# Attention and two expert layers on one core: four more score tiles turned by DMA, and a new written-out order of work

## The chip, the cores and the metric

One core of a Trainium2 chip runs one program. The metric is the device time of one execution in microseconds (us); it is compared as a median of several executions.

## What is computed

The reference first does clustered attention for 2 batches, 8 heads, 768 positions, head size 64, and then two dense layers on the 1,536 tokens.

```python
mask = q_assign[:, :, :, None] == k_assign[:, :, None, :]
scores = scale * np.matmul(q, k.transpose(0, 1, 3, 2))
scores = np.where(mask, scores, -1000000000.0)
scores = scores - np.max(scores, axis=-1, keepdims=True)
attn = np.exp(scores)
attn = attn / (np.sum(attn, axis=-1, keepdims=True) + 1e-09)
return np.matmul(attn, v).astype(np.float32)
...
h = x @ w_in
g = np.where(pos, h, np.where(neg, 0.0, (h + beta) ** 2 / (4.0 * beta)))
return (g @ w_out).astype(np.float32)
...
a = x @ w1
b = x @ w2
h = a * b @ w3
return (h @ w_out).astype(np.float32)
```

`q_assign` and `k_assign` are the nearest of 16 cluster centres; the mask lets a query see the keys of its own cluster alone.

## The kernel before, in words

**The score tiles.** The two batches of attention run one after the other. Each batch has 4 pairs of heads (units), each unit two groups of queries `g`, each group 2 heads `h` with 3 tiles `t` of 128 queries by 768 keys: 48 tiles a batch, numbered `s`, 0 to 47 and 48 to 95. One tile goes through these steps:

- `s` on TensorE (`s_mm`, L846 to L855): eight matmuls into a PSUM bank pair of the ring `sc`.
- `smax` on VectorE (`s_max`, L861), `sbias` on GpSimd (L866), `sexp` on ScalarE (`s_exp`, L874).
- The tile must then be turned, so that keys lie on partitions. `by_pe(s)` (L883) says how. If it is true, `spT` on TensorE (`s_pT`, L891) turns it as six blocks of 128 by 128 into the same bank, and then `shi` (ScalarE or VectorE, `copy`, L347 or L349) writes the upper half in f16 into `pt`, and `sT` on VectorE (`s_lo`, L352) the lower half. If it is false, `shi` and `slo` first write the two f16 halves into a buffer `phl`, and `sT` (`s_T`, L921) turns both by one DMA issued on SyncE's queue (SP) into `pt`.
- `pv` (L962 in the first batch, L970 in the second) multiplies the six turned tiles of a group with the values.

In batch 0 every tile is turned by TensorE, in f32. In batch 1 it is every sixth, that is `h = 0, t = 0` of each of the eight groups: tiles 48, 54, 60, 66, 72, 78, 84 and 90.

**Buffers.** In batch 1 the ring `sc` has two members (L175), so a tile's matmuls wait for the lower half (`slo`, or `sT` on VectorE) of the tile two before it. The ring `phl` has two buffers (L211 and L213); the values `v` of each unit use it too (`vh`, `vlo`, `vT` L772). A buffer of `phl` is free again when its DMA has landed.

**The rest.** While batch 1 of the attention runs, TensorE also does the dense layers of the first batch's tokens (steps `h`, `y`, `ab`, `o`: `mm4`, L1254, twelve matmuls each), and VectorE, ScalarE and GpSimd rebuild 64-bit weights into f32 (L1107 to L1140) and split values into two parts. SP carries the put-back of rebuilt weights (`wd<-wf`, L1143), loads of q, k and v, and all DMA turns. After the attention only dense layers are left (L1254, L1507).

**The order.** Every step is one `plan.add(...)`, 3,072 in all. `Plan.order` (L126) does not plan: it reads the string `ORDER`, two letters a step, which give the step's number and which of its allowed engines runs it. The steps are emitted in that order, and every engine and every DMA queue works strictly in order. So the string alone sets the order on each engine, and the costs and due times in the `add` calls are not used when the kernel is built.

```python
            i, alt = divmod(LETTERS.index(a) * len(LETTERS) + LETTERS.index(b), 2)
            name, engines, _, fn, needs, _, _, prev, _, _ = self.ops[i]
            out.append((fn, list(engines)[alt], name, 0.0))
...
    def by_pe(s):
        return s % PE_EVERY[s // NU] == 0
...
                if by_pe(s):
                    add(("spT", s), {"PE": 0.655}, p + 3.0, s_pT(s, b), [("sexp", s), "c_put"], frees=[(("P", b), s)], near=(("sc", b), s))
                    add(("shi", s), hi, p + 3.5, s_hi(s, u, g, h, t), [("spT", s)], first, behind=key)
                    add(("sT", s), lo, p + 4.2, s_lo(s, u, g, h, t), [("shi", s)], frees=[(("sc", b), s)])
                    continue
                add(("shi", s), hi, p + 3.3, s_hi(s, u, g, h, t), [("sexp", s)], [(("phl", b), s)])
                add(("slo", s), lo, p + 4.0, s_lo(s, u, g, h, t), [("shi", s)], frees=[(("sc", b), s)])
```

Of the kernel before, what the change touches and what calls it, by code (L numbers as in the profile page):

```python
# [35 lines left out]

LETTERS = "#$%&()*+,-./0123456789:;<=>?@ABCDEFGHIJKLMNOPQRSTUVWXYZ[]^_`abcdefghijklmnopqrstuvwxyz|~"
ORDER = (
    "##$V$.$0$4#%#*$X$2#,#0$]#.$Z%s%X%V%Z#(%e#2#4%h%k$6%c$_%y&,%r:m%_$H$8%m$::|$a;.$<%a;<$q%|$c$>%i#_$J&%#i#e$e%u"
# [4 lines left out]
    "+a&G+e+u*s+g&/+V+c,(<g&=,4<L+m,*&4<N<w+w%@<o,6+y,,+|<:,8<i,.<<,@,:<>,#<y<|,<,%<@,0<]<k,L,2<_<P=*,B=:,N,>,D,F"
    ",P=#=%,R&I=(,X<a,H<m<c,u,J<q+i=L,w-4+k&J,Z,y=,<s-6,]=],|+o-8=.=k,_=0=2&N=4,T,W&D-#=6,e=<&T,a-(&Q,g=N=8,c-*-%"
    "=>-,+r=_=|+s-.=a=@&@-:=P=B-@=D-<&B=R-0=F=V=c=T,m&_=H-B=X&Z-2-D>4->=e=g&L&S=i>D&W-L=J=m-F-X=p&c,i-N&k-u&X,l-H"
    "-Z&o=Z&j>R-]=u=q-P-_=s-R-K=w,o-a>#-w>6-T=y>%-V-y>(,q>*-|>,>.-c>8,s%>&e>F>T>H>:>>.(><&].#.*>]-m>V.%.,>X>c>u>Z"
    ">0>J..&b>L-e.0&g>N-g.4>P.@%B>@.6%(-i%%.L-k>_>2.2>B.N?%.B.P.8.:.<-o.D&u&n.F>e>w.H?,.X>z.R>a.Z.J>g?:?J.].>>i._"
    ">k>m.T>q>|.u>o.V.e%*?#.a?]>s?(/(.w?D/4&r.c.g?*/*&y?.($/,&w?0&~-q-s(,?<?m/@/..m/B(%/6?L.y%,((?2/8?4.|%D?N/:?P"
    "?6?_/#?R?8/</%?>/0?@&s?T%./2?B?V/>?a?F?g%F%0?|%2/D/F?H?c?o%H@2@D%4?e?i?q/H?X/L/J?Z%6%J.i.k/N/P/X@,?k.o(*%L/R"  # L50
    "/Z@#.q%N/]/_@%/T.s/e/a/V@(?s%P@T/c%8?u/u?w0(%:@*@.?y/m@4%R%</w%T@6/y@8/g/|0*@F0,04@V@H0#0@06@c@N@:08@00%@J0:"
    "@<@X@>0.@L(.@Z@P0B00@A@m0<@]@s@B/i02@_0LA,/l@a@e0X0N@R0Z0P0R@g0]0?A<0D@i0_@k0T/o@o0a0F0u/q@u0H0w@q0J@w@yAJ0V"
    "0e0d0gA./sA>@|0y0|A#A@1((0A%AB(41#(2A0(61LA6AL0mADAF1*1%1,A2A4A8A(1.10A*ANAH1NAZAP1PAR14120i16AT1@F40l1X180o"
    "AV1:A:1B(:1Z1D(8(=1]1F(A0q1H(>A]1<(DA_AX1?1_AaAm1RAc(BAe1e1JAg(M1g1TB2(HAj1a(N1W1c1iAo2*(G0s1uArBPF>1m2,(J1w"
    "2.20(PAk1y1|2#22B5Bo24BRAs1kBT2%261o1r1s(R28Au(ZB62((TB%(VAx2:(X2FB(AyB+B8A|2<B,C42>B/2HB0Bc2@2JB:2BB<2L2DB>"
    "BDBACR2NBCBrBe2P2TBgB$BV2RBiBFBtC62VBHCq2cBXBJ2XBlB[2ZC(2eBm2]D%2_2gBuFPC8FkB]2i2aCUB_3%2kBa(]CFC*3(CVC,2mBw"
    "By3*C.2o34CsB|3,BMC:BO36CHD4CKC#Cv3.38CX30CLC%C<32C>CNC@3B3:2qC1CwC3D(3<3D(_3FDBCe(gCz3>3H3@3J(a(c3PDP2y3RCZ"
    "3L3TC]CgD+3ND6C_3VD8CB3X3mC|Ci3ZD#D,(i(l3](nCk3_(e3oD03a3q3sD/3c(tDoD>3eDE(u3gDGDLCQFu3|E42sD23iCn3k3vCoD:DN"
    "DR3wD@Cb3yDUCc4>DqD=ER2u(o4@404BDc424D(qCE44(w4FDsDH464H4#De(yDg2xEq48E62|4L4:4JE9DV4NF%F6Di3#4PF8F:Dl4%DX4*"
    "F<DZDKETF@4<4R4)Dm4TD]D_EVE(4V(|4,4XFR)#DuE*FTG>4.FVDb)%FX4ZEsFZE,4iEu4]DwF]E:Gi)(DyE.4_D|4aE$4kEX4cE14mE<4e"  # L60
    "E2FmE>4gEFFoEZFqE&E]4oE@FBFsEe)*4qF)E_F*EH4sEJ5:FwEg4uEa4w5<EiFDEcE|ELFyG@4y5>5@EkFGEwEB4|5#EEGB5%GD5,5BGFF_"
    "F0F#5DFaEyH<Gk5F5.GsGH5VGmF,GJ5(Hg),Go5*).Gq5H5XF|GuENFL5J5LH>GwF2Em5ZF.H@FHG$G2EQ)1HqHiHBFNGL)2I*Hk5NEpHDFg"
    "G4HF5]FJ5PHmHoFc5_5RHsG6IDG85TFiGNG%Gy5a)5HHI,5cIa5eHJI.G~G:GPHLG(5gHuG*FeIF5iG,IN5sIH5kI0IJ50G]ILGRI2GTIP52"
    "5uG.5m54I45wHw5oI6Hy5yGVI|G1GXJN6(5q5|H#6*G_)6G=6,GaG[)@H0H%Gc56H(6#Ic58IeJ#)BH|IgIRH2H*J,IiI8GfIkH46DGg)8H6"
    "ImHN6F6.H-Jy6HI#606%66HZJ%HPH/6J62I;I%J(JP);HRITJR)<J*IV6RHTH]6L6TH_)>I<J.I(Ha)DHc6VJ06N68I@646X6ZHe6PHVJTKD"
    "JV6aIoJXIXH86]IqJ2KgI>J|6_6c)F6oIBIs6eIZJZ6gK#K%6iJ5I]K*K(KF6qK,6kJ6KiH;6mKkIuL2KqJ]KH6s6u7#J`K.6>7%J86wJ;I_"
    "6yHXKJJ<7(7*7N6|KLIwKm7,KNLTKoKP7PKsL4Ja7.7RK1707TK3JcL6L8Je)NIy)HKuJgL:LqJi)JJBJDJk7V72J>JFJm6:)LKRJH7XJAKT"
    "7Z)PK4Jo74JJJqL<6<76JsL>7]KVJMJu6@L_JwK6LVK8LX78LZK_K:KwL]7:KXLaM:7<LsK<KyKa7>7_KcKZMV7a7kK]L@7@7cK|LBK>KeK@"
    "7m7eKBM<7oLD7B7g7qM>)TLuM@)R7yLFLwLeL*6BLy7sLc7iL|MDMBM#7HL#MyMF7|L%7uLgN<L(MX7wLI8#LLMZL,M]MHL.LJM%M_8%8.M("
    "L0LN7D8(Li7G)VMJ8*LPM|LR8,8<MaLkMLN>Lm7J)_807L)XN@82NBM*84N#N%N_Mc)bMeN*86M2N(M,N,Lo8>)])[MN8@N.N|888BMh8:8g"  # L70
    "8DNDMRM.NFN0M0M48iODMPN2Na8FNJMU8k8HNcNMMqMiO#Ne)h)cNiO%M6N88X)eMs8mNgNkMkO(8Z)iM8NmNoNV8JNHN:8o8]O*MmONMoN4"
    "8qOF8_OHO,MuNr8uOaMwN6NX8a8wNZ8RO0OJOL8yP*8c8s8L8|)kO29#NN8eOc9%Oe9(9*N^P,NP8NNw8PP.P0OPPF9,9.ORO.8TOgOi90Ns"
    "9F)m)oOk92)qOmO48VOTNS)sPiNyNUP4O<OWP2P6Nu9H9496OXO69JPHPJPLP8PN98OZOoPPO]Q,9LO>O9Or9NP;P=O|OsQNPT9PPkPsPV9:"
    "O_Pm9<Po9>PqOu9@PXO@9BP#9DPuQkQ.OC9cPyQ1P>9eP%9RQPOwQR9g9qP@9TPROy9iPwPZPaO;QXP|Q2PBQ49s9k9uQ(9mQ6Q89VQ:9o9w"
    "Q=:%P]QTQm9]QV9yQoQZPD9|R4:#P_:4:(:*PcPeP(Q#:6Q]:,PgQq:8Q>Q%QsQ*Q_Qu:.QbQwQyQF:0::Q|Q@:2QB:<:BQHR>Qc:>R6:D:@"
    "R9:F:P9XQK:H9[Qg9_9aQeRPRZ:JQE:R:TR#R@:L:VRB:NQiQLR,R%:Y:ZR:RRR.:]R(RT:_RmRwR*R<R1R2RDR^:a:cRF:g:eRJSNRp:iSR"
    "SPRH:kRXRLR`SLRNSyRVSVS|T#S]S0S:SrRrT%RgSURyS`SXTLSaT)RsT4SfT6SjRaSgRjSnR~RuS2T0S5T8SpTNRcT+S#ReSdTDStT;S<T<"
    "U_S?UaS%T3T-T@S(T/RkTUS*TGTWTYTZT?S6S8TPT^SlTaTeTSTiTdS,VqTqTnUcS.TIUhUoTKSFTlUjVsT`TCUfTsSHUlU%UnThS@X*UsTp"
    "S[U(UuSuSCU6VvSDVzTyTuU8SJSxUxU:UyTwU*U<V|U,V2U|VwV%U.W(U0V*X/U@U>V.UBW#UDT|V$W%V9X,UFU#U2UqY<W,V<UJX0V(W<V>"
    "ULUHU4V0W1UTW+W2UNXNW4UVV@W6VBV,X2UXYJVRW.V4WDV:VTUQX4VHURUZX6VJU]W8V6VLX:X<X>VVWJW@VDVXXAXBVZV]WFVFY>V`WNX]"  # L80
    "WBVNVaWPVcY@XPVPVgVeViW>X9XDVkYXXFWVXRVmWRWoWTYBWrVoWeWLXIWZYMXJX_YFYNWgXaYgXmWsYuW;W^YZWiYPYHWuWwXpYwWkY]W_"
    "WmWaXVXqXLYjXsYTWcYkXuXcZ#XTYyZ&Z(Z,YDWHZ+Z0Z2YcWXXeY|WyZ5[.[0W|Y_Z9Z<Z6Z/YRXgZ;XwZDX#]@X%XyXX]NX|Ye[2XiY#X("
    "[4Y(Y%YVY*YqY,[7[9[?[BYbZ@YmYt]B[;[<Y/[R]]YoXZZN[@ZRZH[FY0XkZ?[D[VY2]EY4[IZFY6ZTY8ZB[aY:[K]F]Q[LZP[e]k]S]yZ_"
    "ZV[TZX[OZi[ZZaZlZc]JZmZo]_]|]X]nZf]oZg[c]b[q]T[Q]HZq^)[X^#]Z[s^+^,_2^0ZJ[u^%[wZL[y_4ZZ]c[gZsZ]Zu]V[#^5^9[&]L"
    "[]Zw^.[iZy]u[m^:[k_;[|],]#[(]q]._=^<]%`D^>]0]([*_>^2]*]g^@Z|^6]3_C[,]s^D_6]w_8`F[_]4_G_@^L]e[o^B^H]i]6^R_I]8"
    "`I_V`R_J`a_M`J]:]=_f]>^F_E^V`L^J`T`W_X_O_P^T`N_S^c^X_T`oa#a2^e^N`P_g^Z`X_u^]`c_x^g`f`q`]_y^m^jae^p^q`ga%^__|"
    "^ka(^s^w^u^y`t`k`_as`ZbL`i^|_Z`#_#a4_%___ia7_a`mbNbT_k_]_c_m_o^P_q_s`0`u`%`2`(`4bV`*`6^a`yb]`8_(bY`:_+`-`<b`"
    "a8b[bbbe_,bi`>bkbn`@a*bg_.`Bag_0`.`wa.ajbdcBa:aLbpa<avaNa,a0aHaxa@aka>cD`|aBaPbPaSaoaKbSaEd8d:amcJayaqcRaGa]"
    "cMb0cOaXb)b#cFb3bqb8cQaacIb:a|d<b%aTd?b4cgc%b+dAbDd]b7d_bsa`bGa[b-byb@dkbwbCbue.cVb/cZcYcuadc_bHdCdEdFc(cUci"
    "cbbKe0ckb<aWccb>c*dHb|f#dmc,cec#c2c]e2dLc.dNcmdPc0c4dJdacydTdRdXc6e7codVc8f(c:cscwe8e>c|e:cqd#e<c<e5dceBc>d("  # L90
    "eFeJc@eDeHeNdof%d%eRfsd,dZd*dgf*d2dedqeVd4d.eLd6ead0fHeAf,dwdidsf.f4dufueTf0dyf8d|f2f<eXf;e#f>e%eZf@eegifVf6"
    "e(fCeggkf|e*e]eQfwg#e,fDfJfLg*eifyemfPecgmekg.g&g(g>eqgrese_fZf]gsfRg2gufXh_gLg1g4fNeufGgBg6fcgwg:gyfgg8eofj"
    "g,hah#ewgoezgFfTg@e|h%f_h4fkg<gPgHfehBhcfag|hggRh(gDhefmgNh8gXfohiiTg]h,h0h6gTg_h/hoh*i*hsfqgah<gJhlhvi.gVh:"
# [1679 lines left out]
```

## Time and profile before

| | |
|---|---|
| median of three runs | 726.48 us (725.79, 726.48, 728.29) |
| the profiled execution, its own time | 725.32 us |
| its span, first to last instruction | 723.6 us |
| granted TensorE clock | 1.00 over the whole span |
| TensorE matmul busy | 704.4 us of the span |
| VectorE, ScalarE, GpSimd busy | 615.9, 465.5 and 285.3 us |

A profile is one execution. Its times count from the span's start. PE is TensorE's matmuls and PEld its weight loads, which overlap them; DVE is VectorE, ACT ScalarE, POOL GpSimd, SP SyncE, which here only issues DMAs. The shape of a tile stands as partitions x elements. A matmul's end is modelled and lies after the start of the next one, so what an engine's piece of work costs TensorE is read from start to start, not from its duration. A bracket at the end of a timeline row is the idle time of that engine just before, and who ended it.

### The profile page before, as it was taken

How to read it: one execution, taken by the hardware profiler on the slowest of the kernel's cores; microseconds unless marked ns; L12 is line 12 of the kernel's file. 1: busy time of each engine (PE TensorE's matmuls, PEld its weight loads, DVE VectorE, ACT ScalarE, POOL GpSimd, SP SyncE). 2: the span in 40 equal slices, each digit the busy share in tenths (PEclk: the TensorE clock that was granted, in tenths of full speed). 3: DMA queues.
4: the chain of work that ended last, by engine and by line, in shares of the span. 5: the costliest groups of instructions: out<-in, count | busy, mean ns of one | idle time of the engine just before them, and what ended most of it. 6: DMA issues, size and time to landing. Idle time of an engine off the chain costs nothing.

```text
span 723.6 us, 11965 instructions
## 1 busy us (share of the span) xinstructions
PE 704.4 (97%) x4144; PEld 617.9 (85%) x4145; DVE 615.9 (85%) x1134; ACT 465.5 (64%) x870; POOL 285.3 (39%) x358
## 2 busy tenths in 40 slices
...
GB/s 312 135 193 131 194 192 272 202 191 201 205 166 199 171 175 217 233 235 187 244 217 225 205 230 157 186 164 152 46 103 57 59 88 59 44 72 74 73 52 80
DMA packets 113932, 115.80 MB, mean 160 GB/s; under 512 B 74128, under 2 KB 82768, under 8 KB 113872
## 3 DMA queue, kind: packets, MB, share of 16 engines
...
q14 instruction: 28, 0.23, 0.1%
...
## 4 chain that ended last, share of the span: by engine, by line
PE 89%; DVE 4%; ACT 3%; DMA 2%; issue 1%; SPq 0%; POOL 0%; ACTq 0%; POOLq 0%; DVEq 0%
PE mo L1254 36%; PE sc L1507 9%; PE sc L853 9%; PE mo L1198 7%; PE mo L1507 5%; PE sc L891 5%; PE sc L1254 5%; PE av L962 4%; PE av L970 3%; PE av L1507 2%; PE av L1254 2%; DMA vn<-phl 1%; DMA kq<-in_qT_dram 1%; DVE nm L861 1%; ACT pt L347 1%
## 5 line engine op out<-in xcount | busy, mean ns | idle before, releaser
L1254 PE MATMUL mo<-X,whl 128*128 128x384 f32 x924 | 169.5, 338 | 0.0
L1254 PEld LDWEIGHTS mo<-X,whl 128*128 128x128 f32 x924 | 159.5, 188 | 2.3 <-issue 0.6
L1254 PE MATMUL mo<-G,whl 128*128 128x384 f32 x732 | 133.2, 337 | 0.0
L1254 PEld LDWEIGHTS mo<-G,whl 128*128 128x128 f32 x732 | 126.6, 188 | 0.9 <-DVE X L352 0.3
L861 DVE TENSOR_REDUCE nm<-sc 128x1 f32<-128x768 f32 x96 | 90.2, 952 | 15.9 <-PE sc L853 13.6
L352 POOL TENSOR_TENSOR whl<-wf,whl 128x512 fp32r<-128x512 f32 x48 | 63.3, 1319 | 73.1 <-ACT whl L347 44.6
L1140 POOL TENSOR_TENSOR wf<-wf,w 128x512 int32<-128x512 int32 x32 | 42.2, 1320 | 80.4 <-DVE wf L1123 32.1
L866 POOL TENSOR_SCALAR nm<-nm 128x1 f32<-128x1 f32 x96 | 26.3, 274 | 102.9 <-DVE nm L861 94.2
L347 ACT ACTIVATE whl<-wf 128x512 fp32r<-128x512 f32 x76 | 47.5, 627 | 29.4 <-PE mo L1254 11.8
L853 PE MATMUL sc<-k,q 128*128 128x512 f32 (+1 forms) x192 | 55.1, 368 | 3.8 <-DVE nm L861 1.6
L1198 PE MATMUL mo<-wo,wf 128*128 128x512 f32 x128 | 58.0, 596 | 0.0
L874 ACT ACTIVATE P<-sc,nm 128x768 f32<-128x768 f32 x56 | 50.1, 898 | 10.6 <-POOL nm L866 5.5
L347 ACT ACTIVATE pt<-sc 128x768 f32<-128x768 f32 (+1 forms) x50 | 39.4, 807 | 18.6 <-PE sc L891 14.7
L853 PE MATMUL sc<-kq 80*128 80x512 f32 (+1 forms) x192 | 49.7, 340 | 0.0
L891 PEld LDWEIGHTS sc<-ident,P 128*128 128x128 f32 x336 | 37.9, 141 | 12.5 <-issue 4.9
L1107 ACT ACTIVATE wf<-w 128x512 f32<-128x512 f32 x64 | 42.4, 672 | 5.7 <-POOL wf L1140 1.7
L891 PE MATMUL sc<-ident,P 128*128 128x128 f32 x336 | 43.9, 275 | 1.6 <-DVE nm L861 1.3
L1123 DVE SCALAR_TENSOR_TENSOR wf<-w,wf 128x512 uint32<-128x512 uint32 x64 | 44.2, 693 | 0.9
L874 ACT ACTIVATE sc<-sc,nm 128x768 f32<-128x768 f32 x40 | 34.7, 868 | 15.5 <-POOL nm L866 15.4
L1198 PEld LDWEIGHTS mo<-wo,wf 128*128 128x128 f32 x128 | 23.3, 190 | 24.5 <-issue 23.7
L352 DVE TENSOR_TENSOR phl<-sc,phl 128x768 f16<-128x768 f32 x40 | 38.1, 952 | 5.6 <-ACT phl L347 5.2
L853 PEld LDWEIGHTS sc<-k,q 128*128 128x128 f32 x192 | 31.4, 189 | 12.2 <-DVE nm L861 3.0
...
## 6 DMA issues: line engine op xcount, KB each, us to landing
...
```

The source lines that it names most:

```text
L347: nc.scalar.activation(out=out, in_=in_, func=AF.Copy)
L352: (nc.gpsimd if e == "POOL" else nc.vector).tensor_tensor(out=out, in0=a, in1=b, op=ALU.subtract)
L853: nc.tensor.matmul(ps[:, n], q[0:n_rows, q0:q0 + 128], k[0:n_rows, n], start=first, stop=not first)
L861: nc.vector.tensor_reduce(out=nm, in_=T[("sc", b), s], axis=AX.X, op=ALU.max, negate=True)
L874: nc.scalar.activation(out=new(("P", b), s).rearrange("p n s -> p (n s)") if by_pe(s) else T[("sc", b), s], in_=T[("sc", b), s], func=AF.E ...
L891: nc.tensor.transpose(T[("sc", b), s][:, c], p[:, c], ident)
L1107: nc.scalar.activation(out=T["wf", i], in_=T[w64, i].bitcast(F32)[:, :, 1], func=AF.Abs)
L1123: nc.vector.scalar_tensor_tensor(out=w, in0=T[w64, i][:, :, 1], scalar=0xC0000000, in1=w, op0=ALU.bitwise_and, op1=ALU.bitwise_or)
L1140: nc.gpsimd.tensor_tensor(out=w, in0=w, in1=T[w64, i].bitcast(I32)[:, :, 0], op=ALU.add)
L1198: nc.tensor.matmul(acc, w[:, k4 * 128:(k4 + 1) * 128], wo2[:, hf * 4 + k4], start=(hf == 0 and k4 == 0), stop=(hf == 1 and k4 == 3),)
L1254: nc.tensor.matmul(acc, w[:, a, k4 * 128:(k4 + 1) * 128], rhs(c, k4), start=(first and k4 == 0 and n == 0), stop=(last and k4 == 3 and n = ...
L1507: nc.tensor.matmul(ps, lhs(av, a, k), rhs(bv, c, k), start=k == 0 and n == 0, stop=k == 1 and n == 2,)
```

## The change

`PE_EVERY` goes from (1, 6) to (1, 12): in batch 1 tiles 48, 60, 72 and 84 are still turned by TensorE, and 54, 66, 78 and 90 go the other way, through `phl` and a DMA. The string `ORDER` is another one throughout.

```diff
-    PE_EVERY = (1, 6)
+    PE_EVERY = (1, 12)
...
 ORDER = (
-    "##$V$.$0$4#%#*$X$2#,#0$]#.$Z%s%X%V%Z#(%e#2#4%h%k$6%c$_%y&,%r:m%_$H$8%m$::|$a;.$<%a;<$q%|$c$>%i#_$J&%#i#e$e%u"
...
+    "###%#>#*#,#0#.$0$V%X%Z$.%V#(#2#4$6$X$2$4$_%e%h%c%r:m%|&#$8$:$a$<$c$>$H#P$Z$]$q#y#6#]#e#i#Z$(%y&,%]:|%_%k&%;."
...
```

Read by the rule of `Plan.order`, both strings hold 3,072 steps. TensorE has 529 steps before and 525 after (the four `spT`), DMA 175 and 179 (four `sT`), VectorE 1,093 both times, ScalarE 931 and 921, GpSimd 344 and 354: some 300 steps that may run on either of two engines have changed theirs. The order within each engine differs in many places by a few steps. At the start SP's loads of q and k come as q0, k0, k1, k3, q1, k2, q3, q2 before and as k1, q0, k0, q1, k2, k3, q2, q3 after (the number is the unit). The last step on TensorE is the same.

## Rows read from the trace of the kernel before

**Rows 1.** The page: busy time of the engines, and the chain that ended last
```profile
PE 704.4 (97%) x4144; PEld 617.9 (85%) x4145; DVE 615.9 (85%) x1134; ACT 465.5 (64%) x870; POOL 285.3 (39%) x358
...
PE 89%; DVE 4%; ACT 3%; DMA 2%; issue 1%; SPq 0%; POOL 0%; ACTq 0%; POOLq 0%; DVEq 0%
```

**Rows 2.** Busy time by stretch; last three columns: granted clock, DMA share, GB/s
```profile
core 0: us, PE busy (x) PEld busy (x) DVE busy (x) ACT busy (x) POOL busy (x), PEclk, DMA share, GB/s
0.00:40.00 40.00, 27.19 (x183) 19.68 (x184) 31.54 (x69) 32.37 (x50) 14.35 (x24) 1.00 0.62 213
40.00:200.00 160.00, 158.52 (x834) 97.20 (x834) 142.86 (x238) 127.48 (x220) 48.14 (x73) 1.00 0.62 200
200.00:480.00 280.00, 278.53 (x1758) 262.25 (x1757) 246.36 (x421) 199.43 (x368) 119.35 (x142) 1.00 0.85 200
480.00:700.00 220.00, 220.00 (x1260) 218.94 (x1259) 190.85 (x403) 104.11 (x231) 100.88 (x117) 1.00 0.26 79
700.00:723.60 23.60, 20.16 (x117) 19.84 (x115) 4.27 (x7) 2.10 (x4) 2.59 (x2) 1.00 0.22 78
```

**Rows 3.** Timeline of PE: start us, us, what; the two waits after 200 us
```profile
279.27 0.62 PE L853 MATMUL sc<-k,q 128*128 128x512 f32 x2 [0.84 <-DVE phl L352]
...
391.53 0.61 PE L853 MATMUL sc<-k,q 128*128 128x512 f32 x2 [0.63 <-DVE phl L352]
```

**Rows 4.** Timeline of PE at the turns of tiles 54 and 78
```profile
225.15 0.82 PE L891 MATMUL sc<-ident,P 128*128 128x128 f32 x6
225.73 2.35 PE L1254 MATMUL mo<-X,whl 128*128 128x384 f32 x12
...
352.55 0.82 PE L891 MATMUL sc<-ident,P 128*128 128x128 f32 x6
353.12 0.60 PE L853 MATMUL sc<-k,q 128*128 128x512 f32 x2
```

**Rows 5.** Groups by line: halves of tiles (count | busy us, mean ns | idle before)
```profile
L352 DVE TENSOR_TENSOR phl<-sc,phl 128x768 f16<-128x768 f32 x40 | 38.1, 952 | 5.6 <-ACT phl L347 5.2
L347 ACT ACTIVATE phl<-sc 128x768 f16<-128x768 f32 x38 | 30.6, 808 | 3.3 <-DMA vn<-phl 1.8 <-DMA pt<-phl 0.8
...
L352 DVE TENSOR_TENSOR pt<-sc,pt 128x768 f16<-128x768 f32 x8 | 7.6, 949 | 2.5 <-ACT pt L347 2.4
```

**Rows 6.** The line that turns score tiles by DMA (duration ns min/median/max)
```profile
L921 SPq DMA_TRANSPOSE pt<-phl x40: 1274/1618/3282, 200.5 to 465.4; - x40
...
DMA to landing us min/median/max: 3.6/5.1/8.4
```

**Rows 7.** DMA queues, 465.3 to 470.4 us (packets, MB, share of 16 engines)
```profile
q1 hardware_dynamic: 1644, 0.41, 42.0%
...
pt<-phl SPq DMA_TRANSPOSE x1, 4.9
```

**Rows 8.** Chain of waits from 262 to 284 us, in order of time
```profile
267.12 10.21 DMA vn<-phl
...
277.41 0.82 ACT phl L347
...
278.25 0.97 DVE phl L352
...
279.27 0.97 PE sc L853 x4
280.24 3.82 PE mo L1254 x22
```

**Rows 9.** Timeline of ACT at tile 64
```profile
277.41 0.81 ACT L347 ACTIVATE phl<-sc 128x768 f16<-128x768 f32 x1 [1.80 <-DMA vn<-phl]
```

**Rows 10.** Timelines of PE and DVE: tile 63, last matmuls to lower half
```profile
268.15 0.51 PE L853 MATMUL sc<-kq 80*128 80x512 f32 x2
...
272.23 0.96 DVE L352 TENSOR_TENSOR phl<-sc,phl 128x768 f16<-128x768 f32 x1
```

**Rows 11.** Timeline of PE in the first 40 us
```profile
10.06 2.32 PE L533 MATMUL sc<-kq,cT 128*32 128x384 f32 x14 [0.43 <-DMA kq<-in_qT_dram]
```

More of the change, by code (lines that the diff above doesn't have):

```diff
@@ L44 @@
[L44 to L93, printed above, removed]
@@ L94 @@
-    "hwhDiVhFh~i_hqiXi9gZgci#hHh>hmhyiqi&i,geh2hNi4iahRi(hJhTi2ggi|hVj4i]i<i>hLith@iZividiDj>i:i0iyhPiHhXiJj#h[jP"
-    "iLj%i@iBi6iFiNiwieiQh]iRikj(imj7jAj9j:ihiiioj.j0jSj+jZjTj2jCj,j<jXj]j_jVjJjLjNjDjgjjjkjajGjHjcje"
+    "###%#>#*#,#0#.$0$V%X%Z$.%V#(#2#4$6$X$2$4$_%e%h%c%r:m%|&#$8$:$a$<$c$>$H#P$Z$]$q#y#6#]#e#i#Z$(%y&,%]:|%_%k&%;."
+    "%m$J%s%u$%$e$s$g$i$L$m%i;<:o:q:w$k:s$@$D$B$N#H#N#@#T#s#q#g%a$F)u$*$##8;H;#%w%o:u:y#:$P)w$R$u;0&()y)|#X*#$,#m"
+    "#_;X;>;J*%;%$o;($w;*$y$|;,;g$T;@;2*(#w#F***4;R;8*,*.&*;Z;i;4%#;B;L;6;:*6*8#J#u#c#R*@*B*D#|*0#B*L;k;m;];D;N;o"
@@ new lines @@
+    ";q;s;F*:*<#a*F#k*H#L*2*>*N*P#o*X*Z#<#D#V*u*];u<(*J*R*T+(;_;a;c;e;P*_*a*e*V*c;w+4*m;T<*&0<6<2*w*g*y*|<B+6+8+*"
+    "+,<,;y;|<#+:+.<R+#+L+%<8+0+<+2<.&7<%&3<0<4+@+N+P+B+D*i*k*o<D<e<T+X+Z+];V+R+F+H+T+><u+_+u+J+V&:+a+c*r<V*s&/<X"
+    "<F<:<Z<L<<<H&=<J<N+w+y,4,(,*+m<g&4+|<],6&9,@,#<i%(<w,,,.,8,:,0,<<><k,%<@<y=*<o=:=L<m+e<|<q,L,B,D+g,N,P,2,>,F"
+    "<P&F=],H,R,J=#=%&E<b&><_=(<c&J&H,u,X,Z,]+i+l,w+o,T-4-6,W=,=/=0=2<s=4=V=k,_-(-*,y-8,|&N-#,a=<=>=@,e=N-:=_=P=B"
+    "=D=F&Q=6=a&U+q+s,c-%,g-,-.=8=H=J&c&@-@-<-0&B,m&W=R-B&M&^-D=c=e=|-2>4->=m=T=X=g=i-X-L-Z-],i,l,o=o-N-P-F-H&e,r"
@@ new lines @@
+    "=Z&R=u>D>R&Z-J-u-R-_-T-a=q=s&l=w=y&_>#-V>6>>-c-w-y-|-e-g,s>%>(>*&p>,>.&b>F>H>J>T>V>c>].(.*>8>:>L>X>N>P&X.#.%"
+    "%*%>%%%B.,..>0-m><>@>2&g-i-k>u>Z.4.0.2.6.8>_.L.@.B.D.N.:&i&v&n>B.<.F.H>e?,?:>w?%>g.X.Z>i>y&r>|>k.J.P.R.>.]>m"
+    ">o?#?(-o?J._>a>q.T.V.a.u.w.y%@>s/4?.?0?]?2&y&|/(/6/*/,/8?*-q-s?4(%.|.c&w(-/:(#%,/.?6?8.e()%D.g/@/B/D?<?L?m?_"
+    "?>?@.m/#?a?N?P?R?T?V?|?D?B?F?c/%/</0/2/>%.%0?e%2?g?i@2/F%F%H%4%6%J?o?r?s&s@D?H@T?X/H/J/L/N/P.i.k/X/Z%L.o?u?w"
+    "?y?k@,@#/R/T@N/].q/_%N.s@%@(@*@.%8/V@c/a/c%P/u/w/y/m@4%:%<?Z%R%T@F@H@6@J@8@:@</e/g(*/|0(040#060%@s080*0,@V@X"
@@ new lines @@
+    "0:0.@L@P@ZA,(.@>@0@A@B0@0B0D@]@_@a@e@g000<02/i/k0L0N0P0F0X0Z@i/o0]@R0?@k@mA<@o0R/q/sA60u0w0y@uA.@w@yA0A2@|A#"
+    "A%(4AJAZ0|0H0T0J0W0_0eA>A@ABADAFAH@qA)0a0c1((0(21#1L1%AT0m1*1,A4A80gAL1NANF41.10120i140k1@1XA:APARAV16181:1<"
+    "1B1D(6A*(:(<(8(>(C1Z1]1P1F1H0o0q(M0sA]AmA_AaAcAeAg(A1>B21_1R1e1g(NAXAj1J1T1W(DAo1a1cAr(G(H(JAkBPB41i1k1u2*1w"
+    "1y1|2,2.20B6Bo(P(R231m1oBS241qC41sBU2#2%26(T2((V(XAsAuAwB%B(282:B*B,AyB/A~2F2HCRBqFP2<2>B8B$2@B:2B2D2JB<2LB>"
+    "B0Bt2N2P2RBcBeBgB@BBF>BiBkFkBD2T2VBVBn2XBFBIBJ2c2e2Z2^BX(Z2_2a(]BZBMC6CTC(CqC*C,B]B`C.BOBuBwByB|BbC$2gC83%3("
```

43 lines of the change are left out of this document (39 added, 4 removed).

## The prediction

> **What bounds the kernel now.** First the page: TensorE's matmuls are busy for 97% of the span, VectorE for 85%, and 89% of the chain that ended last is TensorE [rows 1]. A share over the span hides stages, so next comes the table by stretch [rows 2]. The granted clock is 1.00 in all of them. From 200 to 480 us, the second batch of the attention beside dense layers of the first, TensorE is busy for 278.53 of 280 us. From 480 to 700 us it is busy for 220.00 of 220. So a microsecond that TensorE needs less before 480 us is carried to the end unchanged. Idle time lies at the ends (12.8 us in the first 40, 3.4 in the last 23.6) and in the two waits that make up the 1.47 us missing in the middle, 0.84 and 0.63 us, both on VectorE's `phl` [rows 3]. VectorE is the second engine in that stretch: 246.4 of 280 us, 88%. The DMA engines stand at 0.85 there, against 0.26 afterwards.
>
> **The change part by part.** *Four turns leave TensorE.* A turn is six 128x128 matmuls. Their own times overlap, so the price is from their start to that of the next matmul: 0.58 us for tile 54, 0.57 for tile 78; tiles 66 and 90 show 0.57 as well, the same pattern [rows 4]. Together 0.58 + 3 x 0.57 = 2.29 us. TensorE is the engine that never rests there, so the whole of it is on the path: minus 2.3 us.
>
> *Halves of the tile.* Upper and lower half are written either way. VectorE's lower half takes 0.949 us into `pt` and 0.952 into `phl` [rows 5], so four tiles change by 0.01 us: nothing. The upper half reads the same PSUM tile and writes as many f16 numbers; ScalarE's 0.808 us stands for both. The exponential now goes back into PSUM and not into `P`; ScalarE rests for 80 of the 280 us [rows 2] and hides that. If VectorE were full, this step would still add nothing, because VectorE's instructions are only moved: between the maxima of tiles 50 and 95, VectorE has 385 steps in the old string and 381 in the new one.
>
> *Four DMA turns are added on SP.* Each holds SP for 1.62 us (1.27 to 3.28) and lands 5.1 us after its issue (3.6 to 8.4) [rows 6]. One turn takes SP's DMA queue 42.0% of 5.1 us on all 16 engines, 2.1 us [rows 7]; four take 8.6. The DMA engines then stand at (0.85 x 280 + 8.6) / 277.7 = 0.89. Behind a turn on SP stand put-backs of weights, q and k loads for later units and the next turns. What hides the four: each is the first tile of its group, and the `pv` that reads it comes after five more tiles of its group. I cost them at nothing on the path. From below there is no gain to expect of them; from above, the bound is 4 x 1.80 us, from the worst wait for a `phl` buffer that ScalarE shows (below).
>
> *The two `phl` buffers get four more users.* This is the cover that can go. With 40 tiles and 4 values a buffer is claimed 44 times in some 265 us [rows 6], then 48 times. The trace shows what one late turn does: the turn of the values of unit 5 took 10.21 us to land, ScalarE's upper half of tile 64 stood behind it, then VectorE's lower half, then the matmuls of a later tile that needed the bank [rows 8]. ScalarE lost 1.80 us [rows 9], TensorE 0.84 [rows 3]. On the other side, a tile turned by DMA gives its PSUM bank back without waiting for a slot on TensorE. That is a gain which I can't price beyond the 1.47 us of idle time that exists.
>
> *The order.* On TensorE most steps move by a few places. The tightest pair I find in the new one is tile 92 and tile 94, which share a bank: between them stand one score tile and two `ab` steps, some 5.1 us of TensorE (0.97 + 2 x 2.08; 22 matmuls of L1254 last 3.82 us, so twelve 2.08 [rows 8]). Tile 63 shows that the way from the last matmul to the lower half can be done in 273.19 - 268.66 = 4.53 us [rows 10]. So it fits with 0.6 us to spare if VectorE and ScalarE run the tile at once; the new order puts two 0.5 us steps and one maximum between. In the old order a `pv` and a third `ab` step stood between the two as well. At the start the load of q1 goes from fifth to fourth among the loads of q and k, and TensorE waited 0.43 us for a q load [rows 11]: a gain between 0 and 0.43 us. I take 0, since VectorE's chain of small steps follows. About 300 steps change engine between VectorE, ScalarE and GpSimd; their bounds are a gain of the 1.47 us of waits and a loss of as much again or more. I take 0, as the number of VectorE's steps is the same.
>
> *Sum.* -2.3 us of TensorE, 0 for the rest. The profiled execution took 725.32 us, 1.7 us more than its span; it would become 723.0. It stands 1.16 us under the median of 726.48, so against the median the forecast is 726.48 - 2.3 = 724.2 us.
>
> **A rule against it.** What the rows show is 0.57 us of TensorE against 5.1 us from issue to landing for the same tile [rows 4, 6]. The Trainium skill, "VectorE: DVE Perf Modes", Rules for kernel authors, says that a 128x128 block is to be turned by TensorE where PSUM will do as the target, and by DMA only otherwise. Followed here it would keep the four turns; if a DMA turn's time stood on the path, the sum would be 4 x (5.1 - 0.57), or 18 us slower. The rows speak against that as a whole, since a turn has tens of microseconds until its `pv`; by way of the buffers it can still come true in part, and this is the fourth case.
>
> **The rivals.** *Case 1, the forecast*: TensorE's 2.3 us come through with 1 us of scatter, 723.2 to 725.2 us. For it: no idle TensorE from 480 to 700 us.
>
> *Case 2, given back*: the new order has more waits of the kind there are now, from one of 0.84 us to three of some 0.73 (the mean of 0.84 and 0.63): 724.2 + 0.8 to 2.2 = 725.0 to 726.4 us. For it: VectorE at 88% over the stretch, the DMA engines at 0.89, and the pair 92 and 94. Against it: such waits were only two in 280 us before.
>
> *Case 3, more than the turns*: the two waits go, and the start gains its 0.43: 724.2 - 1.47 - 0.43 = 722.3 us. For it: banks come back sooner for four tiles. Against it: neither wait stood at a tile that is changed.
>
> *Case 4, slower*: the two `phl` buffers become the bound around tiles 54, 66, 78 and 90. A wait of ScalarE for a buffer then passes to VectorE and the PSUM bank in full, 4 x 1.80 = 7.2 us: 731.4 us. It decides from (2.2 + 2.3) / 4 = 1.1 us lost by TensorE per tile. For it: the one late turn in rows 8, and the DMA engines near full. Against it: that wait cost TensorE 0.84 us, less than 1.1.
>
> That the change would not do what it says is left out: four `spT` are gone from the string, and four `sT` stand on DMA.
>
> **How the numbers follow.** About 0.3%, or 2.2 us, is what a measurement of this kernel can tell from no change; the bounds are 724.3 and 728.7 us. Case 1 gets 0.41; its middle lies at the bound, 0.24 below and 0.17 above. Case 2 gets 0.23, all of it no change; case 3 0.17, faster; case 4 0.19, slower. So faster 0.41, same 0.40, slower 0.19. The likeliest time is 724.2 us. The range reaches from a little under case 3, 721.6, to the lower part of case 4, 729.5; outside lie some 0.05 below and 0.13 above. Case 1's own range is 723.2 to 725.2.
>
> **What would show it.** Right: 24 matmuls of L891 fewer, 44 DMA turns of L921, TensorE's busy time in the stretch of the attention's second batch 2.3 us less with no more than 1.5 us idle, and 480 to 700 us still full. Case 2 and 4 would show as idle time of TensorE before L853 with `phl` as releaser, case 4 with ScalarE waiting for `pt<-phl` close to the four tiles and landings over 5.1 us in the median. Case 3 would show no such wait at all. If TensorE idles after 480 us, or the start loses or gains over 1 us, the order and not the turns has made the difference, and the forecast's reason is wrong whatever its number.

## The result, and the profile after

The changed kernel takes 734.45 us (median of 4 executions, 732.06 to 735.2) beside 726.13 us for the kernel before on the same chip: a ratio of 1.0107 as recorded, 95% interval 1.0082 to 1.0132 (the quotient of the two medians is 1.0115). It is 1.1% slower; the forecast was 724.2 us, and the range ended at 729.5.

The profiled execution took 734.55 us, its span is 732.5 us, the mean granted clock 0.993. The page of the kernel after, first the engines' busy time, then the share of the chain that ended last:

```profile
PE 707.6 (97%) x4120; PEld 619.0 (85%) x4121; DVE 620.7 (85%) x1134; ACT 456.6 (62%) x860; POOL 297.5 (41%) x368
...
PE 83%; DVE 8%; ACT 3%; DMA 3%; issue 2%; POOL 1%; SPq 0%; ACTq 0%; DVEq 0%
```

TensorE runs 24 matmuls fewer than in [rows 1] and is busy for 3.2 us longer, and its share of the chain falls from 89% to 83%. Fewer matmuls that take longer are a first sign of the clock. The table by stretch of the kernel after (columns as in [rows 2]):

```profile
0.00:40.00 40.00, 28.36 (x184) 20.67 (x185) 32.92 (x69) 31.68 (x49) 14.82 (x24) 1.00 0.62 213
40.00:200.00 160.00, 155.80 (x801) 96.09 (x802) 138.34 (x232) 121.58 (x211) 50.41 (x72) 0.98 0.58 194
200.00:480.00 280.00, 275.00 (x1707) 256.60 (x1708) 249.19 (x424) 201.00 (x374) 121.21 (x144) 0.99 0.93 206
480.00:700.00 220.00, 219.29 (x1269) 216.83 (x1266) 191.16 (x394) 98.82 (x224) 108.51 (x126) 1.00 0.27 81
700.00:732.50 32.50, 29.15 (x169) 28.83 (x167) 9.11 (x18) 3.49 (x7) 2.58 (x2) 1.00 0.21 73
```

Against [rows 2], TensorE's idle time grows from 1.48 to 4.20 us between 40 and 200 us, where no tile is turned otherwise than before, and from 1.47 to 5.00 us between 200 and 480 us. In the same two stretches the granted clock is no longer 1.00. The DMA engines stand at 0.93 where 0.89 was forecast.

**The first place, tile 31, in batch 0.** The timeline of TensorE in the kernel after, around the longest wait:

```profile
121.86 0.52 PE L853 MATMUL sc<-kq 80*128 80x512 f32 x2
125.24 1.01 PE L853 MATMUL sc<-k,q 128*128 128x256 f32 x2 [2.87 <-POOL q L352]
126.05 0.84 PE L853 MATMUL sc<-kq 80*128 80x256 f32 x2
```

The chain of waits there names what TensorE waited for:

```profile
122.41 0.71 ACT kq L347
...
123.39 1.81 POOL q L352
...
125.24 1.65 PE sc L853 x4
```

These are `qh(3,1)` and `qlo(3,1)`, the writing of the queries of unit 3, head 1. Read by the rule of `Plan.order`, the new string puts tile 32 ahead of tile 31, then those two writes, then tile 31. Both tiles belong to unit 2, head 0. Tile 32 is listed as that head's last reader, so behind it the head's buffers `q1` and `kq2` go to unit 3, head 1, and tile 31, which reads the same buffers, has to wait until the next head's numbers are in them. (It computes with them: in part, tile 31's scores, and tile 58's below, are made from another head's queries or keys. In the kernel before this holds for tiles 19, 58 and 67; TensorE has no idle time in front of any of the three.) In the old string tile 31 stands ahead of both writes.

The granted clock behind that wait, in the table by stretch of the kernel after (the third row is half slow, half fast; the last is the third place, below):

```profile
110.00:124.00 14.00, 12.38 (x57) 7.82 (x55) 11.62 (x18) 11.03 (x20) 4.36 (x8) 1.00 0.94 326
125.00:130.00 5.00, 4.76 (x8) 2.60 (x9) 2.88 (x4) 3.03 (x5) 1.08 (x3) 0.50 0.15 44
130.00:132.00 2.00, 2.00 (x4) 0.86 (x3) 1.59 (x3) 1.96 (x4) 0.00 (x0) 0.59 0.00 0
...
368.00:370.00 2.00, 2.00 (x8) 1.91 (x7) 1.96 (x5) 1.84 (x5) 0.00 (x0) 0.50 0.75 206
```

From 124.8 us on, while TensorE is still waiting, the clock is 0.50, that is 1.2 GHz in place of 2.4, for 6.83 us. TensorE works for 6.4 us of these at half speed, which costs 3.2 us. The wait of 2.87 us thus costs 6.1 on the spot.

**The second place, tile 58.** Timeline of TensorE in the kernel after:

```profile
247.81 0.62 PE L853 MATMUL sc<-k,q 128*128 128x512 f32 x2 [1.57 <-DVE k L352]
```

The same pattern: tile 59 ahead of tile 58, and between them `kh` and `klo` of unit 5, head 1, which go into the buffer that tile 58 reads. In the old string, too, tile 58 stands behind `kh`, but ahead of `klo`, for which TensorE waits here, and there it did not wait. Here the clock stayed.

**The third place, tile 78, one of the four changed.** The chain of waits of the kernel after:

```profile
353.28 10.16 DMA pt<-phl
...
363.54 0.97 DVE phl L349
364.53 0.96 DVE phl L352
365.48 0.47 DVE tmp L1279
...
366.09 3.29 PE mo L1254 x12
```

The turn of tile 76 takes 10.16 us to land. Tile 78's halves want that `phl` buffer, and the new string puts the upper half, too, on VectorE. VectorE works in order, so the drain of a dense step (L1279) stands behind both halves. The timelines of VectorE, ScalarE and TensorE of the kernel after show it passing on:

```profile
363.54 0.96 DVE L349 CAST phl<-sc 128x768 f16<-128x768 f32 x1 [3.74 <-DMA pt<-phl]
```
```profile
365.98 0.53 ACT L347 ACTIVATE G<-tmp 128x384 fp32r<-128x384 f32 x1 [3.47 <-DVE tmp L1279]
```
```profile
366.09 3.29 PE L1254 MATMUL mo<-G,whl 128*128 128x384 f32 x12 [2.69 <-DVE tmp L1279]
```

3.74 us of VectorE become 2.69 us of TensorE, and behind that the clock is 0.50 for 3.41 us, another 1.7 us lost.

**The account.** Waits of 2.87, 1.57, 2.69 and one more of 0.69 us at 337 us, less the two of [rows 3] that do not come again, make 7.82 - 1.47 = 6.35 us. The low clock costs 3.2 + 1.7 = 4.9. Four turns save 2.3. The sum is 8.95 us; the spans differ by 732.5 - 723.6 = 8.9. That it is so close is in part luck: by the two pages TensorE's idle time grew by 5.7 us, where the waits give 6.35, and its busy time by 3.2, where the clock less the turns gives 2.6. Differences of under 1.3 us at the start and after 480 us about cancel.

### The profile page after: what moved, and what is told of

Same layout as the page of the kernel before. It is cut to its first block, busy times and chain, and to the rows that moved or that the text cites. A ratio compares the mean times of both kernels' runs of the same rounds, so it can differ in the third digit from the quotient of the medians.

```text
span 732.5 us, 11938 instructions
## 1 busy us (share of the span) xinstructions
PE 707.6 (97%) x4120; PEld 619.0 (85%) x4121; DVE 620.7 (85%) x1134; ACT 456.6 (62%) x860; POOL 297.5 (41%) x368
## 4 chain that ended last, share of the span: by engine, by line
PE 83%; DVE 8%; ACT 3%; DMA 3%; issue 2%; POOL 1%; SPq 0%; ACTq 0%; DVEq 0%
PE mo L1254 33%; PE sc L853 9%; PE mo L1198 8%; PE sc L1507 7%; PE sc L1254 6%; PE mo L1507 5%; PE av L962 4%; PE sc L891 4%; PE av L970 3%; PE av L1507 2%; DMA pt<-phl 1%; DMA kq<-in_qT_dram 1%; PE av L1254 1%; DVE nm L861 1%; ACT pt L347 1%
## 5 line engine op out<-in xcount | busy, mean ns | idle before, releaser
L1254 PE MATMUL mo<-X,whl 128*128 128x384 f32 x912 | 166.4, 337 | 0.1
L1254 PE MATMUL mo<-G,whl 128*128 128x384 f32 x696 | 128.1, 338 | 2.7 <-DVE tmp L1279 2.7
L1254 PEld LDWEIGHTS mo<-G,whl 128*128 128x128 f32 x696 | 121.3, 189 | 4.1 <-issue 3.0
L352 POOL TENSOR_TENSOR whl<-wf,whl 128x512 fp32r<-128x512 f32 x46 | 60.8, 1326 | 51.3 <-ACT whl L347 21.9
L347 ACT ACTIVATE whl<-wf 128x512 fp32r<-128x512 f32 x72 | 44.9, 627 | 47.0 <-PE mo L1254 18.5
L874 ACT ACTIVATE P<-sc,nm 128x768 f32<-128x768 f32 x52 | 46.6, 899 | 12.8 <-POOL nm L866 6.9
L874 ACT ACTIVATE sc<-sc,nm 128x768 f32<-128x768 f32 x44 | 38.3, 870 | 21.7 <-POOL nm L866 19.7
L352 DVE TENSOR_TENSOR phl<-sc,phl 128x768 f16<-128x768 f32 x44 | 41.9, 952 | 4.2 <-ACT phl L347 3.8
L891 PEld LDWEIGHTS sc<-ident,P 128*128 128x128 f32 x312 | 35.5, 141 | 11.4 <-issue 5.1
L891 PE MATMUL sc<-ident,P 128*128 128x128 f32 x312 | 40.6, 274 | 2.3 <-ACT P L874 1.9
```

The lines of the kernel that those rows point to most:

```text
L347: nc.scalar.activation(out=out, in_=in_, func=AF.Copy)
L352: (nc.gpsimd if e == "POOL" else nc.vector).tensor_tensor(out=out, in0=a, in1=b, op=ALU.subtract)
L874: nc.scalar.activation(out=new(("P", b), s).rearrange("p n s -> p (n s)") if by_pe(s) else T[("sc", b), s], in_=T[("sc", b), s], func=AF.E ...
L891: nc.tensor.transpose(T[("sc", b), s][:, c], p[:, c], ident)
L1254: nc.tensor.matmul(acc, w[:, a, k4 * 128:(k4 + 1) * 128], rhs(c, k4), start=(first and k4 == 0 and n == 0), stop=(last and k4 == 3 and n = ...
```

## The experiments

In the first four kernels the string `ORDER` is cut into lines of another length, so their line numbers are one lower than above. A diff of the string is given by the names of the steps. The kernel before ran beside each set: 726.36 us (18 executions) beside the first four, 726.48 (32) beside the next four, 726.6 (23) beside the last two.

### One place mended: tile 31

```diff
-s 32, ..., qh(3,1), qlo(3,1), s 31
+s 32, ..., s 31, qh(3,1), qlo(3,1)
```

> The changed kernel, but tile 31's matmuls are emitted ahead of the two steps that write unit 3's queries (head 1) into the buffers tile 31 still reads; the order on each engine stays as it is. Theory of places: the loss of the changed kernel lies in a few waits, and the largest is TensorE's 2.87 us at 122 us plus 6.83 us right behind it at a granted clock of 0.5, which cost half, 3.4 us. Both go: 734.4 - 6.3 = 728.1 us, and the granted clock stays at 1.00 from 100 to 160 us. Rival, contention: the four more DMA turns, between 200 and 480 us, make the loss; then this edit changes less than 1 us. Rival, order as such: the wait at 122 us moves to another step near by, and the gain stays under 3 us.

Measured: 735.0 us (732.97 to 737.65), ratio 1.0123 [1.0096, 1.0151]. No gain, which is the number that the rival, contention, had given. Timeline of TensorE and table by stretch in this kernel:

```profile
243.52 0.62 PE L852 MATMUL sc<-k,q 128*128 128x512 f32 x2 [1.57 <-DVE k L351]
...
365.15 4.18 PE L1253 MATMUL mo<-G,whl 128*128 128x384 f32 x12 [3.75 <-DVE tmp L1278]
```
```profile
245.00:247.00 2.00, 2.00 (x8) 2.00 (x7) 1.97 (x3) 0.81 (x2) 0.37 (x2) 0.50 1.02 214
...
366.00:368.00 2.00, 2.00 (x8) 2.00 (x7) 2.00 (x5) 1.41 (x4) 0.89 (x2) 0.50 0.91 129
```

The wait and the low clock at tile 31 are gone, and at tile 47 this kernel is 4.3 us ahead of the changed one (its first matmul starts at 183.24 us in place of 187.53; 6.3 us were expected); contention alone would not have put it ahead there. But now the clock falls behind the same 1.57 us at tile 58, the wait at tile 78 is 3.75 us, and the clock is low for 6.83 us there. The saving at one place was given back at the other two. The theory foresaw the saving and missed its fate: the costs of the places do not simply add, since the price of a wait depends on whether the clock falls behind it, and for how long.

### One place mended: tile 78

```diff
-        return s % PE_EVERY[s // NU] == 0
+        return s % PE_EVERY[s // NU] == 0 or s == 78
```

In the string the turn by TensorE takes the place of tile 78's upper half, the upper half (by ScalarE) that of the lower, and the lower half that of the DMA turn.

> The changed kernel, but tile 78 is turned by TensorE again, its three steps in the same places of the order. Theory of places: VectorE's 3.74 us before tile 78's upper half (a phl buffer still under a DMA that took 10.16 us to land), TensorE's 2.69 us behind it and 3.41 us at a granted clock of 0.5 go; the turn costs 0.57: 734.4 - 2.7 - 1.7 + 0.6 = 730.6 us, granted clock 1.00 from 340 to 400 us. Rival, contention: a quarter of the added turns goes, so a quarter of the loss of 8.3 + 2.3 us, 2.6, comes back less 0.6: 732.4 us, with the wait still there. Rival, order as such: +0.6 us, 735.0.

Measured: 731.15 us (728.58 to 738.33), ratio 1.0093 [1.0055, 1.0132]. The median is near the theory of places, but the seven executions spread over 10 us, and the interval, some 730 to 736 us, holds both rivals as well: the time does not decide. The profile, of the quickest of the seven, does for this one execution. The waits of 2.87 and 1.57 us stand as before, in its timeline of TensorE:

```profile
124.64 0.88 PE L852 MATMUL sc<-k,q 128*128 128x256 f32 x2 [2.87 <-POOL q L351]
...
245.71 0.62 PE L852 MATMUL sc<-k,q 128*128 128x512 f32 x2 [1.57 <-DVE k L351]
```

From 340 to 400 us TensorE has no idle time at a clock of 1.00, so none stands near tile 78. Where the long executions wait has no profile.

### All four tiles back to TensorE

```diff
-    PE_EVERY = (1, 12)
+    PE_EVERY = (1, 6)
```

> The new order with all four tiles turned by TensorE again: the order alone, without the change of way. Theory of places: 734.4 - 4.4 (tile 78's wait and the clock behind it) + 2.3 (four turns) = 732.3 us, with the wait and the low clock at 122 to 132 us still there. Rival, contention: near the kernel before, 726 to 727 us. Rival, order as such, in which the turns do save 2.3 us: 736.7 us.

Measured: 746.47 us (741.02 to 747.49), ratio 1.0265 [1.0227, 1.0302]: far off all theories, and no evidence on the order alone. The turn was put where the upper half had stood, with no step of TensorE between the exponential and it at tiles 54 and 66, so TensorE, working in order, waited for ScalarE there (1.28 and 3.56 us). From its timeline of TensorE, the worst of these:

```profile
290.88 1.54 PE L890 MATMUL sc<-ident,P 128*128 128x128 f32 x6 [3.56 <-ACT P L873]
```

What it does show is that a change of the way can need other steps moved with it: at tile 78 the same edit made no wait. Waits and the clock account for this kernel, too. In its profile the waits of over 0.6 us after the first 40 are 13.0 us in all and the clock is low for 17.1, half of it lost; less the 1.47 of [rows 3] that is 20.1, and its span is 20.4 us longer than the kernel before's.

### The four DMA turns in the old order

```diff
-    PE_EVERY = (1, 6)
+    PE_EVERY = (1, 12)
```

> The old order with the four tiles 54, 66, 78 and 90 turned by DMA, their steps in the places of the old ones: the change of way alone. Theory of places: 726.1 - 2.3 = 723.8 us if no tile meets a phl buffer that is not free, and up to 4.4 us more for each that does (a wait of 2.7 us and the clock behind it); no wait at 122 us. Rival, contention: 732 us or more, without any single wait over 1 us. Rival, order as such: 723.8 us.

Measured: 727.66 us (724.89 to 733.24), ratio 1.0023 [1.0001, 1.0044]. The turns alone neither gain their 2.3 us nor cost the 8 us of the change. Chain of waits and timelines of ScalarE and TensorE at tile 78:

```profile
350.17 5.24 DMA pt<-phl
...
355.44 0.73 ACT phl L346
```
```profile
355.44 0.81 ACT L346 ACTIVATE phl<-sc 128x768 f16<-128x768 f32 x1 [1.32 <-DMA pt<-phl]
```
```profile
357.78 1.49 PE L1253 MATMUL mo<-G,whl 128*128 128x384 f32 x7 [1.34 <-DVE tmp L1278]
```

Even with a landing of 5.24 us, near the median of [rows 6], tile 78 meets an occupied buffer; here ScalarE waits for it, 1.32 us, and TensorE loses 1.34, for a step of the drain stands behind on ScalarE. The profile also has a wait of 1.91 us at 133 us with a low clock behind it, in batch 0 and before any changed tile; its chain goes back to a weight transfer that took 9.73 us, and no tile goes by DMA there.

### Both late readers mended

```diff
-s 32, ..., qh(3,1), qlo(3,1), s 31
+s 32, ..., s 31, qh(3,1), qlo(3,1)
...
-s 59, ..., kh(5,1), ..., klo(5,1), ..., s 58
+s 59, ..., s 58, kh(5,1), ..., klo(5,1)
```

> The new kernel with two entries of its order moved: tile 31's scores ahead of the writing of unit 3 head 1's queries, tile 58's ahead of the writing of unit 5 head 1's keys; every operation keeps its engine. Theory of places: TensorE's waits of 2.87 us (tile 31) and 1.57 us (tile 58) and the low clock behind them go; the wait at tile 78 stays (2.69 us and a low clock of 3.41 to 6.83 us, which costs half its length). Lost time up to 260 us of the span then stands within 1 us of the kernel before's, and the whole run is 734.4 less 5.0 less 2.1, 727.3 us, or 729 if the clock falls for 6.83 us at tile 78. Theory of the order as such (waits come up elsewhere in the same sum): 733 or more, with new waits of over 1 us before 260 us. Theory of DMA turns alone: no change but at tile 78, and TensorE's time before 260 us as in the new kernel, 734.

Measured: 727.43 us (725.47 to 730.38), ratio 1.002 [1.0001, 1.0038], the theory of places almost to the digit. Two steps out of 3,072 take back 7.0 of the 8 us. What is left is tile 78, in this kernel's timeline of TensorE:

```profile
359.29 3.82 PE L1254 MATMUL mo<-G,whl 128*128 128x384 f32 x12 [2.33 <-DVE tmp L1279]
```

### All three places mended

The edit of the kernel above, and `or s == 78` in `by_pe`.

> The kernel new_order_31_58_early with tile 78 turned by TensorE as in the kernel before (one TensorE turn of 0.58 us more). Theory of places: none of the three waits and no low clock behind them; 734.4 less 5.0, 2.1 and 4.4, plus 0.6, is 723.5 us, below the kernel before (726.4) by about the three turns that TensorE is spared and the two waits of 0.84 and 0.63 us that the new order does not have. Theory of the order as such: 728 or more, with other waits in the place of these. Theory that every DMA turn of tiles 54, 66 and 90 costs TensorE what it spares: 725.5, the two waits alone being gained.

Measured: 724.14 us (722.91 to 724.6), ratio 0.9967 [0.995, 0.9984]: faster than both kernels, and within 0.7 us of what the theory of places said. The string now has no reader behind the next head's write. The table by stretch of this kernel:

```profile
40.00:200.00 160.00, 158.35 (x827) 97.00 (x829) 143.25 (x239) 123.54 (x216) 51.66 (x77) 1.00 0.61 199
200.00:480.00 280.00, 278.41 (x1751) 262.01 (x1750) 246.81 (x420) 199.32 (x369) 120.69 (x140) 1.00 0.90 208
```

TensorE is full again in both stretches and the clock is 1.00; it was so in all 12 executions (0.999 in one). That is most of the gain: of the 32 executions of the kernel before beside it only 13 had a clock of 0.999 or more, and their median is 725.04 us, 0.9 above this kernel's in place of 2.3. Landings are no quicker here, the longest takes 12.5 us, and ScalarE waits behind one. Its timeline:

```profile
299.34 0.81 ACT L347 ACTIVATE phl<-sc 128x768 f16<-128x768 f32 x1 [2.88 <-DMA pt<-phl]
```

TensorE's one wait near it is 0.62 us, for `phl`. So it matters where a late landing strikes: VectorE waiting 3.74 us with a drain behind it cost 2.69 us, ScalarE waiting 2.88 us here cost 0.62 at most. Not the engine alone decides, for ScalarE's 1.32 us at tile 78 in the old order passed on in full.

### Three DMA turns in the old order

`PE_EVERY = (1, 12)` with `or s == 78`, in the old order.

> The kernel before in its own order, with tiles 54, 66 and 90 turned by DMA and tile 78 left to TensorE. Theory that the one late landing (tile 78's, 1.34 us of TensorE's waiting in old_order_four_by_dma) gave the gain back: no wait of over 0.9 us between 200 and 480 us, and 726.4 less three turns of 0.58 us, 724.7 us. Theory that DMA turns cost TensorE elsewhere about what they spare, whichever tiles they are: 726 to 728 again.

Measured: 725.54 us (722.97 to 728.3), ratio 0.9985 [0.9965, 1.0005]. That is 0.8 us above the first theory and under the second. Against four turns, on another chip, it is 2.1 us less, which points to tile 78 for the loss. Against the kernel before, 0.94 us are saved where three turns are worth 1.7; the interval holds no gain at all, so the rest stays open. The kernel with all three places mended turns the same tiles in the same ways; its median is 725.54 - 724.14 = 1.4 us lower, which is what the new order is worth without its three faults. It seems to be worth that by the clock: the four of these 12 executions in the old order that had a clock of 0.999 or more have a median of 724.05 us, and the mended order kept the clock in 12 of 12.

### The fault planted in the old order

```diff
-s 31, ..., s 32, ..., qh(3,1), ..., qlo(3,1) on VectorE
+s 32, qh(3,1), qlo(3,1) on GpSimd, s 31
```

> The kernel before with the fault of the new order planted at one place: tile 32's scores ahead of tile 31's, and between them the writing of unit 3 head 1's queries, the low half on GpSimd, so that tile 31's scores (reading other queries, a part of the computation that is changed) wait for these writes. All tiles are turned as in the kernel before. Theory of places: TensorE waits 2 to 4 us at some 125 us before tile 31's scores, and where the granted clock falls to 0.5 behind it, for 3.41 or 6.83 us, half of that more: 726.4 plus 2.9 plus 1.7 to 3.4, that is 731 to 733 us; 729.3 if the clock stays. Theory that the order as a whole, not this place, made the new kernel slow: within 1 us of 726.4.

Measured: 730.87 us (728.96 to 733.47), ratio 1.0058 [1.0035, 1.0082], 4.4 us more than the kernel before. Timeline of TensorE and table by stretch:

```profile
126.46 0.88 PE L853 MATMUL sc<-k,q 128*128 128x256 f32 x2 [2.88 <-POOL q L352]
```
```profile
127.00:130.00 3.00, 3.00 (x6) 1.59 (x6) 1.85 (x3) 2.28 (x4) 0.78 (x2) 0.50 0.74 223
```

The same wait to 0.01 us, and the clock low for 3.41 us behind it: 2.9 + 1.7 = 4.6. Three steps are enough to plant it, with all tiles turned as before.

### Tile 78 again: whose lateness is it?

The kernel with both late readers mended, but tile 76 turned by TensorE (`or s == 76`) and 78 by DMA.

> The kernel new_order_31_58_early (727.43 us, 2.33 us of TensorE's waiting at tile 78) with tile 76 turned by TensorE and tile 78 still by DMA: one TensorE turn more, as in new_order_three_places_mended (724.14 us), but the changed tile 78 keeps its DMA turn. Tile 78's halves then go into the phl buffer that tile 75 had, not the one that waits for tile 76's late landing. Theory that tile 78's wait is the wait for a phl buffer whose last turn landed late: no wait of over 0.9 us between 340 and 380 us, 724 to 725 us. Theory that the DMA turn of tile 78 itself (its place in the order, its traffic) costs TensorE the time: a wait of 2 us or more near 360 us again and 727 to 728 us.

Measured: 725.14 us (724.33 to 729.14), ratio 0.9986 [0.9967, 1.0004]. Timeline of TensorE where the wait had stood:

```profile
360.80 0.51 PE L853 MATMUL sc<-k,q 128*128 128x512 f32 x2
...
361.50 4.33 PE L1254 MATMUL mo<-G,whl 128*128 128x384 f32 x24
```

No wait. With as many DMA turns, and tile 78's among them, the loss is gone once the turn before it in the same buffer is. So what cost the time was the wait for tile 76's landing, not the turn of tile 78.

Whether the added turns or the new order delay that landing, the profiles of the other kernels tell. Tile 76's turn alone, issue to landing, in the kernel before and in the one of the new order whose four tiles are all turned by TensorE:

```profile
pt<-phl SPq DMA_TRANSPOSE x1, 4.8
```
```profile
pt<-phl SPq DMA_TRANSPOSE x1, 8.7
```

In the four profiles of the old order it takes 4.8 to 5.3 us, with the added turns or without; in the seven of the new order in which it goes by DMA, 8.7 to 12.6. The delay came with the order. What in the order makes it is not shown.

The last kernel leaves all four turns to DMA and writes tile 78's halves behind 16 more steps (18 places, with the two that move along):

> The kernel new_order_31_58_early with the writing of tile 78's two halves and its DMA turn moved down the order by 18 steps (some 3 us of TensorE's work later), all four turns by DMA, engines unchanged. Theory that the wait hurts because VectorE, which works in order, stands still for the phl buffer with the drains of four matmul steps behind it: the drains pass first, TensorE's wait at 359 us (2.33 us) falls to under 1 us and the clock stays, unless tile 79, which needs tile 78's bank, waits in its place; 727.43 less 2.33, less 1.7 for the low clock, and with one TensorE turn fewer than new_order_three_places_mended 723.5 to 724.5 us. Theory that a late landing costs TensorE its time wherever the halves stand: 727 us or more, with TensorE waiting for tile 78's halves or bank.

Measured: 729.08 us (724.61 to 735.03), ratio 1.0036 [1.0006, 1.0065]. By the median the first theory missed by 4.6 us, and the second one's 727 us or more came true. The profiled execution, 726.19 us, has the smaller wait that the first had foreseen:

```profile
361.07 0.61 PE L853 MATMUL sc<-k,q 128*128 128x512 f32 x2 [0.72 <-DVE phl L352]
```

But the executions spread over 10 us. Those at a clock of 0.999 or more took 724.6 to 729.2, those below 729.0 to 735.0. There is no profile of a long one, so where they wait stays open, and with it which of the two theories holds.

## Why the prediction was wrong

**Four turns leave TensorE: the matmuls are gone, and the account bears the 2.3 us.** The row of L891 in the page after counts 312 matmuls, 24 fewer. By itself the saving was not seen: in the old order three turns brought 0.94 us of 1.7, with an interval that reaches past no gain.

```profile
L891 PE MATMUL sc<-ident,P 128*128 128x128 f32 x312 | 40.6, 274 | 2.3 <-ACT P L874 1.9
```

**Halves cost nothing: right in size, wrong in place.** VectorE's halves of tile 78 take 0.97 and 0.96 us in the chain. But the new string puts both on VectorE, and the text counted VectorE's steps without asking which of them may have to wait, and what stands behind.

**DMA turns at nothing on the path: right at three tiles.** The line of the DMA turns in the kernel after, to set beside [rows 6]:

```profile
L921 SPq DMA_TRANSPOSE pt<-phl x44: 1274/1528/4265, 206.3 to 472.1; - x44
...
DMA to landing us min/median/max: 3.6/4.4/11.5
```

The median landing is shorter, the longest longer, and neither decided. The longest of these, tile 65's 11.5 us, held up ScalarE alone, in its timeline

```profile
305.68 0.81 ACT L347 ACTIVATE phl<-sc 128x768 f16<-128x768 f32 x1 [1.91 <-DMA pt<-phl]
```

and TensorE has no wait of 0.5 us near it. No `pv` waited long for a turned tile, as the prediction said; the claim on the buffer did. Tile 78 cost 2.1 us more by DMA than by TensorE in the old order and, with both late readers mended, 727.43 - 724.14 = 3.3 in the new one, by way of its buffer. The rule of the Trainium skill, "VectorE: DVE Perf Modes", Rules for kernel authors, by which TensorE would have kept the four turns, came true at this one tile.

**Two `phl` buffers: case 4 was the right mechanism, at one tile instead of four.** The price was not 1.80 us but 3.74 of VectorE and 2.69 of TensorE, plus 1.7 for the clock. The bound was taken from ScalarE's worst wait [rows 9], as if it did not matter what stands behind the waiting engine's step. Nor did the added users alone make it: tile 78's claim met a landing that the new order delays. The signs named for case 4, ScalarE waiting for `pt<-phl` close to the four tiles and a median landing over 5.1 us, did not show.

**The order, "I take 0": the step that failed.** It was put at nothing because the number of VectorE's steps is the same, which says nothing of who waits for whom; its bounds were a gain of 1.47 us and "a loss of as much again or more". It cost 2.87 + 1.57 us of waits and 3.2 us of low clock, 7.6 us, and mending just these two places took 7.0 back. The prediction looked for tight pairs of tiles that share a PSUM bank in batch 1, one ring of the many whose buffers the string hands on. Reading for each ring who still reads a buffer after the next head's write finds tiles 31 and 58 in the new string and 19, 58 and 67 in the old one, without a run; which of them wait, and how long, it does not tell, for the three in the old string cost nothing. That the order was to blame was to show as idle time after 480 us or at the start; TensorE was idle for 0.7 us between 480 and 700 us and for 1.2 us less in the first 40, so both signs showed, but the loss stood elsewhere, most of it in batch 0, which the prediction did not look at. Case 3's 1.47 us were in fact gained, for neither old wait came again, though not for its reason: with the four tiles by DMA in the old order a wait of 0.62 us stayed.

**The clock had no term.** The table of before says 1.00 throughout [rows 2], and it was taken as given. That profile was one of those at full clock: 19 of the 32 executions of the kernel before beside the mended kernels had a clock below 0.999, and their median is 727.49 us against 725.04 for the other 13. With 4.9 us it is the second largest item of the account. Without it the change would have cost 4 us, still above case 2.
